# One V piece of the last block requested in two parts, 119 and 9 partitions, in a one-core attention decode kernel

## The chip, the cores and the metric

The kernel runs on one core of a Trainium2 chip. The time is that of the device for one execution, in microseconds, as the median of the runs. A core has TensorE (PE, matrix products; PEld is its weight load), VectorE (DVE), ScalarE (ACT), GpSimd (POOL) and SyncE (SP), which here only issues DMA requests. The requests are carried out by 16 DMA engines, which all move packets from HBM to SBUF, the on-chip memory of 128 partitions.

## The reference

One token attends over a cache of 65,536 positions: 8 heads of K and V, each with 2 query heads, 256 elements per head, bf16. A small gated mixer over the same token is added. Cut to what matters:

```python
q = (x @ wq).reshape(B, Sq, Hq, Dh)                    # 16 heads of 256
scores = einsum("bhqd,bhkd->bhqk", q, k) * Dh ** -0.5  # k, v: 8 heads x 65536 x 256
p = softmax(scores)
a = einsum("bhqk,bhkd->bhqd", p, v).reshape(...) @ wo  # 4096 -> 448
g = sigmoid((x * gate_w).sum(-1))
out = g * a + (1 - g) * mixer(x)
```

K and V together are 537 MB, and each byte is used once per query pair.

## The kernel before

The cache is cut into 32 blocks of 16,384 positions (`NBLK`; four to each K/V head). In a block, partition p holds 128 consecutive positions (`VP`), so a K or V block is 128 partitions x 64 KB, 8 MB. For each block the kernel loads K, transposes it on VectorE (`transposes`, L410), multiplies it with the queries (`scores`, L418), makes the softmax of the block with a running maximum (`softmax`, L475 to L514), and multiplies the probabilities, transposed in `pT`, with V (`pv`, L438). Blocks 0 to 29 run in a loop of 15 rounds with two blocks each (L605); each round also loads and uses the output weights Wo of one head. Blocks 30 (`L - 1`) and 31 (`L`) stand behind the loop, written out.

All large requests are issued by SyncE, in program order (`seq` pins the order on each engine). The 16 DMA engines take them up in that order. Each request counts up one of eight completion counters, taken in turn; before a request is issued, the former request on its counter must have landed.

For the last block, V doesn't go to its usual buffer `vt`, which still holds block 30, but to the K slots that have come free (`v_half`). It is requested by `load_v_last` (L158 to L164) in seven pieces of falling size, all 128 partitions wide: rows j = 0 to 63 of each partition, then 64 to 95, 96 to 111, 112 to 119, 120 to 123, 124 and 125, 126 and 127. A row is 256 bf16, 512 bytes. Behind them SyncE requests the last Wo tile (`load_wo`, L152) and, at the very end, writes the output (L705).

What uses this V: the lower half (j below 64) goes through `pv` into `pv_last` (L438). The upper half goes through `columns` (L463), which makes for each j two products with V as the stationary operand, one for each half of the head's columns, into `hd_ps`. `columns(64, 80)` comes first, then eight products that add the accumulated rest (L684), then `columns(80, 128)`. With the four rows of the changed piece (j = 120 to 123) go eight of these products. Behind them follow a scaling on VectorE (L691), eight products with Wo (L697; the second four use the Wo tile of L152), two copies (L703, L704) and the output.

Of the kernel before, what the change touches and what calls it, by code (L numbers as in the profile page):

```python
# [21 lines left out]
KP = VP // 2  # L22
# [11 lines left out]
def kernel(  # L34
# [15 lines left out]
    nc = tc.nc  # L50
# [12 lines left out]
    def seq(ins):  # L63
        e = ins.ins.engine
        if e in last:
            tc.add_manual_dep(
                ins.ins,
                last[e],
                mybir.DependencyInfo(
                    mybir.DependencyClass.NoSync, mybir.DependencyReason.DATA  # L70
                ),
                reason="program order",
            )
        last[e] = ins.ins.name
        return ins
# [47 lines left out]
    def rows(name, n):  # L123
        return flat[name][bass.ds(n, 1)].rearrange("o p j d -> (o p) j d")
# [15 lines left out]
    v_half = [slots[0], slots[2]]  # L140
    LAST = ((0, 64), (64, 96), (96, 112), (112, 120), (120, 124), (124, 126), (126, 128))

    def load_wo_wide(h):
        seq(nc.sync.dma_start(
            out=wo_in[0:128:WS],
            in_=A_wo.rearrange("(h q c) n -> h q c n", q=128 // WS, c=WC)[bass.ds(h, 1)].rearrange(
                "o q c n -> (o q) c n"
            ),
        ))
# [8 lines left out]

    def load_v_last(n):
        for j0, j1 in LAST:  # L160
            seq(nc.sync.dma_start(
                out=v_half[j0 // KP][:, j0 % KP:(j1 - 1) % KP + 1, :],
                in_=rows("v", n)[:, j0:j1, :],
            ))  # L164

    seq(nc.scalar.dma_start(out=xr[:], in_=A_x[0, 0].rearrange("(o n) -> o n", o=1)))
    seq(nc.sync.dma_start(
        out=wq_t[:, :], in_=A_wq[DM:D, :].rearrange("r (h n) -> (r h) n", h=2)
# [8 lines left out]
    for n0, n1 in ((0, D // 2), (D // 2, D)):  # L177
        seq(nc.scalar.dma_start(
            out=gw[:, n0:n1], in_=gate_w.rearrange("(o n) -> o n", o=1)[:, n0:n1]
# [14 lines left out]
        out=val[:], in_=rowsel[:, :, :, 0:NI], op=ALU.add, axis=AXIS.XY  # L194
    ))
    fst = const.tile([128, 2, REP], FP32)
    for e in range(2):
        seq(nc.vector.tensor_reduce(
            out=fst[:, e, :], in_=rowsel[:, :, :, e:e + 1], op=ALU.add, axis=AXIS.XY
# [3 lines left out]
        out=par[:], in_=ident_f[:].rearrange("p (a r) -> p r a", r=REP), op=ALU.add, axis=AXIS.X  # L203
# [3 lines left out]
        out=nval[:], in0=val[:], scalar1=-scale, scalar2=None, op0=ALU.mult  # L207
# [7 lines left out]
        out=same[:], in_=val[:].unsqueeze(1).to_broadcast([128, 64, REP])  # L215
# [8 lines left out]
        out=sel[:],  # L224
        in_=ident.rearrange("p (w k) -> p w k", w=NW).unsqueeze(2).to_broadcast([128, NW, NQ, 32]),
# [7 lines left out]
        out=xrr[:], in_=xr[:, DM:D].unsqueeze(2).to_broadcast([1, D - DM, 2])  # L233
    ))
    x_col = hd_ps[:, 40:44]
    for k in range(3):
# [13 lines left out]
        out=xtm[:], in0=par[:], scalar1=x_col[:, 3:4], scalar2=None, op0=ALU.mult  # L250
# [19 lines left out]
        out=veps[:], in0=mv[:, 1:2], scalar1=1e-5, scalar2=None, op0=ALU.add  # L270
# [5 lines left out]
    for _ in range(2):  # L276
# [3 lines left out]
            out=ntmp[:], in0=ntmp[:], scalar1=-0.5, scalar2=1.5, op0=ALU.mult, op1=ALU.add  # L280
# [3 lines left out]
        out=h_bc, in0=xf, scalar1=mv[:, 0:1], scalar2=rstd[:, 0:1],  # L284
        op0=ALU.subtract, op1=ALU.mult,
    ))
    for b in range(NF):
        seq(nc.scalar.activation(
            out=gel[b], in_=h_bc, func=ACT.Gelu_apprx_tanh,
# [33 lines left out]
    for k in range(2):  # L323
        seq(nc.vector.tensor_copy(
            out=qq[:, :, :, k, :], in_=qq_ps.rearrange("p (w g r) -> p w g r", g=HKV, r=REP)
# [279 lines left out]
    with tc.For_i(0, HQ - 1, 1, iteration_sync="staggered") as t:  # L605
        for e in range(2):
            if e:
                tc.stage_boundary()
            if e == 0:
                spread_wo(1)  # L610
                head_end()
                older_wo()
            tc.previous_stage_wait(mybir.EngineType.Activation)
            score_block(
                e, (e, e + 1), early_signals(0), FORWARD if e else UPPER_FIRST
            )
            load_v(2 * t + e)
            tc.stage_boundary()
            if e == 0:
                load_k_whole(2 * t + 1, 1)  # L620
                load_wo_wide(t)
                softmax(e, may_begin=True)
                tc.previous_stage_wait(mybir.EngineType.DVE)
                tc.previous_stage_wait(mybir.EngineType.Activation)
                products(e)
            else:
                load_k_whole(2 * t + 2, 0)
                softmax(e, pair=t + 1)
                tc.previous_stage_wait(mybir.EngineType.DVE)
                tc.previous_stage_wait(mybir.EngineType.Activation)  # L630
                denominators()
                turn()
                products(e)
# [6 lines left out]
    for n in (L - 1, L):  # L640
# [4 lines left out]
        if n == L - 1:  # L645
            load_v(n, 0, 48)
            load_k(L, 0, 2)
            load_k(L, 1, 1)
            load_v(n, 48, VP)
        else:  # L650
            load_v_last(L)
            load_wo(HQ - 1, 1)
        if n < L:
            softmax(n % 2)
        else:
            def rest_base():
# [9 lines left out]
                out=lsv[:], in0=val[:], scalar1=lsum[:, 0:1], scalar2=None, op0=ALU.mult  # L666
# [8 lines left out]
                out=rdv[:], in0=rdv[:], scalar1=gcol[:, 0:1], scalar2=None, op0=ALU.mult  # L675
# [6 lines left out]
    for c in range(2):  # L682
# [9 lines left out]
        out=oT[:], in0=o_last, in1=rdv[:].unsqueeze(1).to_broadcast([128, 2, REP]), op=ALU.mult  # L692
# [43 lines left out]
```

## Time and profile before

| | us |
|---|---|
| median of 3 runs | 1264.28 (1263.87 to 1925.72) |
| span of the profiled execution | 1261.8 |
| PE busy | 824.5 (65%) |
| DVE busy | 711.8 (56%) |
| HBM read | 544.22 MB, 431 GB/s over the span |

The span goes from the first to the last instruction of the profiled execution. The queue q1 carries SyncE's requests, q10 those of ScalarE, and q8 and q14 fetch instructions.

### The profile page before, as it was taken

Reading aid. Unit: us, or ns where it says so; the run is one execution under the profiler, and the core shown is the slowest. Engines: PE = TensorE matmul, PEld = TensorE weight load, DVE = VectorE, ACT = ScalarE, POOL = GpSimd, SP = SyncE. Lnnn points to the kernel's source line nnn. Section 1 sums busy time; section 2 is a strip of 40 time slices with the busy share of each in tenths; the row PEclk is TensorE's granted clock in tenths of the full one; section 3 lists DMA queues with packets and bytes.
Section 4 is the critical chain, followed back from the end, with each engine's and each line's share of the span. In section 5 each row is a group of like instructions: output and inputs, shape, how many; then the busy total and the mean of one; then the engine's idle time right before and its main releaser. Section 6 shows DMA issues by size and latency. Waiting matters only on the chain.

```text
span 1261.8 us, 12358 instructions
## 1 busy us (share of the span) xinstructions
PE 824.5 (65%) x4818; PEld 331.2 (26%) x4818; DVE 711.8 (56%) x755; ACT 75.7 (6%) x163; POOL 4.8 (0%) x9
## 2 busy tenths in 40 slices
PE   4757467575666756577566766658656576665668
PEld 2222122222222312223222322223222232222224
DVE  5665456654556644566544665445655456654575
ACT  4000000000000000000000000000000000000000
POOL 1000000000000000000000000000000000000000
PEclk8887788877787877978778887788877797877878
DMA  9999999999999999999999999999999999999998
GB/s 415 435 435 432 439 432 432 437 434 437 432 434 435 434 425 440 416 441 443 423 434 437 432 432 439 432 439 432 432 439 432 439 432 432 439 432 435 421 435 355
DMA packets 11624, 544.36 MB, mean 431 GB/s; under 512 B 1532, under 2 KB 1918, under 8 KB 2782
## 3 DMA queue, kind: packets, MB, share of 16 engines
q1 hardware_dynamic: 11522, 544.22, 99.6%
q8 instruction: 6, 0.10, 0.0%
q14 instruction: 4, 0.03, 0.0%
q10 hardware_dynamic: 92, 0.01, 0.0%
HBM read 544.22 MB, written 0.00 MB: 431 GB/s over the span
## 4 chain that ended last, share of the span: by engine, by line
DMA 67%; PE 14%; DVE 13%; issue 4%; ACT 0%; SPq 0%; DVEq 0%; ACTq 0%
DMA k_all<-in_A_k_cache_dram 67%; PE sc L418 13%; DVE kT L410 13%; PE hd_ps L463 0%; PE pv_last L438 0%; PE pv_last L563 0%; PE f L563 0%; DVE rmax L475 0%; PE hd_ps L684 0%; ACT p_sb L506 0%; PE hd_ps L554 0%; PE pv_ps L438 0%; PE f L697 0%; PE sm_ps L493 0%; DVE pT L513 0%
## 5 line engine op out<-in xcount | busy, mean ns | idle before, releaser
L418 PE MATMUL sc<-kT,qz 128*128 128x512 bf16 x2048 | 550.4, 419 | 315.0 <-DVE kT L410 314.8
L410 DVE STREAM_TRANSPOSE kT<-k_all 128x2048 f32<-128x2048 f32 x256 | 571.3, 2283 | 207.6 <-DMA k_all<-in_A_k_cache_dram 154.7
L418 PEld LDWEIGHTS <-qz 128*128 128x128 bf16 x2048 | 212.5, 104 | 651.3 <-issue 474.8
L438 PE MATMUL pv_ps<-vt,pT 128*4 128x512 bf16 x1968 | 172.0, 525 | 27.3 <-DVE pT L513 27.3
L519 DVE SCALAR_TENSOR_TENSOR acc<-acc,al,pv_ps 128x512 f32<-128x512 f32 x31 | 23.2, 747 | 160.4 <-PE pv_ps L438 160.4
L438 PEld LDWEIGHTS <-pT 128*4 128x4 bf16 x2000 | 56.5, 108 | 130.1 <-issue 83.9
L506 ACT ACTIVATE p_sb<-sc,nb 128x512 bf16<-128x512 f32 x32 | 22.0, 687 | 1020.0 <-DVE nb L502 1020.0
L475 DVE TENSOR_REDUCE rmax<-sc 128x1 f32<-128x512 f32 x32 | 22.1, 692 | 63.7 <-PE sc L418 63.7
L513 DVE STREAM_TRANSPOSE pT<-p_sb 128x512 bf16<-128x512 bf16 x32 | 22.8, 712 | 27.1 <-ACT p_sb L506 27.1
L525 PE MATMUL hd_ps<-lsum,same 128*128 128x1 f32 x30 | 8.2, 342 | 28.8 <-DVE lsum L514 28.8
L493 PE MATMUL sm_ps<-mrun,ones_f 1*128 1x2 f32 x64 | 12.1, 256 | 21.2 <-DVE mrun L492 13.0
L479 PE MATMUL sm_ps<-ident_f,rmax 128*1 128x128 f32 x32 | 8.6, 270 | 24.5 <-DVE rmax L475 24.5
L563 PE MATMUL pv_last<-wo_in,steps 128*128 128x448 bf16 x64 | 15.6, 368 | 5.5 <-PEq L605 5.5
L563 PEld LDWEIGHTS <-steps 128*128 128x128 bf16 x128 | 11.6, 101 | 22.6 <-issue 14.4
L493 PEld LDWEIGHTS sm_ps<-mrun,ones_f 1*128 1x128 f32 x64 | 9.4, 182 | 27.4 <-DVE mrun L492 16.3
L567 ACT CAST wo_sb<-pv_last 128x448 bf16<-128x448 f32 x16 | 8.5, 532 | 126.3 <-PE pv_last L563 126.3
L558 DVE TENSOR_TENSOR a_acc<-a_acc,hd_ps 1x448 f32<-1x448 f32 x15 | 9.1, 608 | 12.3 <-PE hd_ps L554 12.3
L554 PE MATMUL hd_ps<-wo_sb,oT 128*1 128x448 bf16 x60 | 15.8, 351 | 0.0
L563 PE MATMUL f<-wo_in,steps 128*128 128x448 bf16 x64 | 15.5, 367 | 0.0
L570 ACT COPY wo_sb<-wo_sb 128x896 bf16<-128x896 bf16 x15 | 14.1, 937 | 14.5 <-PE hd_ps L554 14.5
L525 PEld LDWEIGHTS hd_ps<-lsum,same 128*128 128x128 f32 x30 | 6.9, 285 | 30.1 <-DVE lsum L514 30.1
L550 DVE CAST oT<-hd_ps 128x2 bf16<-128x2 f32 x15 | 2.4, 160 | 20.8 <-PE hd_ps L540 20.8
(124 smaller groups left out, 194.6 us busy)
## 6 DMA issues: line engine op xcount, KB each, us to landing
k_all<-in_A_k_cache_dram SPq DMA_DIRECT2D x2, 4096.0 KB, 15.2
vt<-in_A_v_cache_dram SPq DMA_DIRECT2D x1, 5120.0 KB
k_all<-in_A_v_cache_dram SPq DMA_DIRECT2D x1, 4096.0 KB
wo_in<-in_A_wo_dram SPq DMA_DIRECT2D x15, 224.0 KB, 27.8
vt<-in_A_wq_dram SPq DMA_DIRECT2D x1, 3072.0 KB, 10.4
vt<-in_A_v_cache_dram SPq DMA_DIRECT2D x1, 3072.0 KB
k_all<-in_A_v_cache_dram SPq DMA_DIRECT2D x1, 2048.0 KB
k_all<-in_A_v_cache_dram SPq DMA_DIRECT2D x1, 1024.0 KB, 21.7
```

The source lines that it names most:

```text
L410: seq(nc.vector.transpose(out=kT_tiles[i % 2][:].rearrange("p j w k c -> p (j w k c)").bitcast(FP32), in_=slots[pair[i // 4]][:, i % 4 * N ...
L418: seq(nc.tensor.matmul(sc_tiles[e][:, :], lhsT=qz[:, 2 * w + c, 2 * (NI - i):2 * (NI - i) + 128], rhs=kT_tiles[i % 2][:, :, w, :, c], star ...
L438: seq(nc.tensor.matmul(dst[32 * grp:32 * grp + 2 * REP, :, :], lhsT=pT[:, 32 * jj + 2 * REP * ip:32 * jj + 2 * REP * (ip + 1)], rhs=pairs( ...
L475: seq(nc.vector.tensor_reduce(out=rmax[:], in_=sc_ps[:, :], op=ALU.max, axis=AXIS.X))
L493: seq(nc.tensor.matmul(sm_ps[:, 128:128 + REP], lhsT=ones_f[0:1, :], rhs=mrun[0:1, :], start=True, stop=True))
L506: seq(nc.scalar.activation(out=p_sb[:, :], in_=sc_ps[:, :], func=ACT.Exp, scale=scale, bias=nb[:, 0:1], accum_out=den[:, 0:1],))
L513: seq(nc.vector.transpose(out=pT[:, :], in_=p_sb[:, :]))
L519: seq(nc.vector.scalar_tensor_tensor(out=acc[:], in0=acc[:], scalar=al_tiles[e][:, 0:1], in1=src[:, :, :], op0=ALU.mult, op1=ALU.add,))
L525: seq(nc.tensor.matmul(hd_ps[:, 460:461], lhsT=same[:].rearrange("p a r -> p (a r)"), rhs=lsum[:, 0:1], start=True, stop=True,))
L554: seq(nc.tensor.matmul(a_ps, lhsT=oT[:, c, r:r + 1], rhs=wo_sb[:, r, c, :], start=(r == 0 and c == 0), stop=(r == REP - 1 and c == 1),))
L563: seq(nc.tensor.matmul(wo_ps[c], lhsT=steps[:, WS - u:WS - u + 128], rhs=wo_in[:, 2 * u + c, :], start=(u == 0), stop=(u == WS - 1),))
L570: seq(nc.scalar.copy(out=wo_sb[:, 0], in_=wo_sb[:, 1]))
```

## The change

The piece of rows j = 120 to 123 is requested in two parts, partitions 0 to 118 and partitions 119 to 127. The other six pieces, all destinations and all computations are the same. The rows of the piece so land under two completion counters, and the requests behind it use the next counter each.

```diff
     LAST = ((0, 64), (64, 96), (96, 112), (112, 120), (120, 124), (124, 126), (126, 128))
 
+    PARTS = {120: ((0, 119), (119, 128))}
+
...
     def load_v_last(n):
         for j0, j1 in LAST:
-            seq(nc.sync.dma_start(
-                out=v_half[j0 // KP][:, j0 % KP:(j1 - 1) % KP + 1, :],
-                in_=rows("v", n)[:, j0:j1, :],
-            ))
+            for p0, p1 in PARTS.get(j0, ((0, 128),)):
+                seq(nc.sync.dma_start(
+                    out=v_half[j0 // KP][p0:p1, j0 % KP:(j1 - 1) % KP + 1, :],
+                    in_=rows("v", n)[p0:p1, j0:j1, :],
+                ))
```

## The prediction

> **What bounds the kernel now.** I read the page first: its span, the row of DMA busy shares, the queues and the shares of the chain.
>
> ```profile
> span 1261.8 us, 12358 instructions
> DMA  9999999999999999999999999999999999999998
> ...
> q1 hardware_dynamic: 11522, 544.22, 99.6%
> ...
> q10 hardware_dynamic: 92, 0.01, 0.0%
> ...
> DMA 67%; PE 14%; DVE 13%; issue 4%; ACT 0%; SPq 0%; DVEq 0%; ACTq 0%
> ```
>
> The 16 DMA engines are busy in every slice, and 544.22 MB take the whole span. The kernel is bound by the stream of K and V, except in the last microseconds, where what the last bytes allow must still be computed. The change touches one of the last requests of that stream, so only the end can move. The span is 1261.8 us and the median of the runs 1264.28 us: 2.5 us lie outside the first and the last instruction, and the change doesn't touch them. Of the three runs two lie 0.41 us apart (1263.87 and 1264.28); the third, 1925.72 us, is no measure of this change.
>
> Next, the chain of waits in order of time, its last 12 us:
>
> ```profile
> 1250.37 0.71 DVE pT L513
> ...
> 1251.88 1.83 PE pv_last L438 x32
> 1253.71 0.89 PE hd_ps L463 x32
> 1254.60 1.07 PE hd_ps L684 x8
> 1255.67 2.55 PE hd_ps L463 x96
> 1258.22 0.02 issue
> 1258.25 0.17 DVE oT L691
> 1258.42 0.04 issue
> 1258.46 0.95 PE f L697 x8
> 1259.42 0.37 DVE res L703
> ```
>
> No DMA stands in it. From pT on, TensorE goes from step to step without a wait that the chain shows. The 96 products of L463 (`columns(80, 128)`, two to a V row j) include the eight for j = 120 to 123, whose rows are the changed piece. The timeline gives their pace, and the start of the very last one:
>
> ```profile
> 1255.53 2.68 PE L463 MATMUL hd_ps<-pT,k_all 128*128 128x2 bf16 x96
> ...
> 1258.05 0.17 PE L463 MATMUL hd_ps<-pT,k_all 128*128 128x2 bf16 x1
> 1258.46 0.91 PE L697 MATMUL f<-wo_sb,oT 128*1 128x224 bf16 x8 [0.25 <-DVE oT L691]
> ```
>
> One product lasts 0.17 us and they overlap: (2.68 - 0.17) / 95 = 26.4 ns from one to the next. At that pace the four products of the last piece (j = 126, 127) start from 1258.05 - 3 x 0.026 = 1257.97 us, and the eight of the changed piece from 1258.05 - 15 x 0.026 = 1257.65 us. Now when the data is there: SyncE's issues of V, and their time to landing (the answer for L161).
>
> ```profile
> 1219.79 17.87 SPq L161 DMA_DIRECT2D k_all<-in_A_v_cache_dram  x7
> 1238.31 0.33 SPq L152 DMA_DIRECT2D wo_sb<-in_A_wo_dram  x1
> ...
> L161 SPq DMA_DIRECT2D k_all<-in_A_v_cache_dram x7: 327/328/424, 1219.8 to 1237.2; - x7
> ...
> DMA to landing us min/median/max: 20.7/21.2/21.7
> ```
>
> The last V request is issued at 1237.2 us, and with 20.7 us it lands at 1257.9 us, some 0.07 us before TensorE comes to it. So two chains end together: the V stream and TensorE's products. This decides the whole forecast: V that comes earlier gains next to nothing, and V that comes later by more than 0.07 us costs its full lateness.
>
> Last, the stages of the tail (columns: stretch, length, busy time and count of PE, PEld, DVE, ACT and POOL, granted clock, DMA share, GB/s):
>
> ```profile
> 1252.00:1254.00 2.00, 2.00 (x46) 0.93 (x39) 0.68 (x4) 0.00 (x0) 0.00 (x0) 1.00 0.97 410
> ...
> 1255.00:1256.00 1.00, 1.00 (x25) 1.00 (x25) 0.00 (x0) 0.00 (x0) 0.00 (x0) 0.91 1.06 403
> 1256.00:1257.00 1.00, 1.00 (x43) 1.00 (x41) 0.00 (x0) 0.00 (x0) 0.00 (x0) 0.50 0.85 312
> 1257.00:1258.00 1.00, 1.00 (x44) 1.00 (x42) 0.00 (x0) 0.00 (x0) 0.00 (x0) 0.50 0.37 134
> 1258.00:1259.00 1.00, 0.75 (x16) 0.44 (x13) 0.16 (x1) 0.00 (x0) 0.00 (x0) 0.50 0.01 4
> ```
>
> In the microsecond to 1256 all 16 engines work; in the one to 1258 the share is 0.37, about 6 of 16. The engines don't finish together: most are done near 1256.5, and some six run on to about 1258. Those late engines set the 1257.9.
>
> **The change, part by part.** It replaces one request (128 partitions, 4 rows of 512 B each, 256 KB) by one of 119 partitions and one of 9. The bytes and their order stay. Everything before the last V requests is the same instruction for instruction, so the loop's time stays.
>
> *One more issue on SyncE.* Two requests of L161 back to back show its price:
>
> ```profile
> 1236.77 0.90 SPq L161 DMA_DIRECT2D k_all<-in_A_v_cache_dram  x2
> ```
>
> Two took 0.90 us, of which one lasts 0.42, so one more costs 0.48 us. It moves the last two V requests from 1236.8 and 1237.2 to about 1237.3 and 1237.7, with about 20 us to go until they land; the queue before them hides it. Without that cover it would cost 0.48 us.
>
> *The completion counters move by one.* The requests take eight counters in turn, and a request waits until its counter's former user has landed. With one request more, the last V request takes over the wait for `vt` that Wo had, and Wo waits instead for the first half of the last V block:
>
> ```profile
> SPq L161 <- DVE kT L410: 22.8, 4, 9.7
> ...
> SPq L152 <- DMA vt<-in_A_v_cache_dram: 0.6, 1, 0.6
> ```
>
> ```profile
> vt<-in_A_v_cache_dram SPq DMA_DIRECT2D x1, 5120.0 KB
> k_all<-in_A_v_cache_dram SPq DMA_DIRECT2D x1, 4096.0 KB
> ```
>
> The last V request so goes out at about 1238.3 us (when Wo goes now), 1.1 us later than now and still 19 us early. Wo (L152) waits for the half block of 4096 KB. The pieces behind that half are another 4096 KB, 4.19 MB at 410 to 430 GB/s = 9.8 to 10.2 us, so it lands about 10 us before 1257.9, near 1248. Wo is then issued near 1248.2 instead of 1238.3, some 8 us before the first engines run out of V (1256). Hidden; without that cover Wo would come as late as its issue is late. Behind it on SyncE stands only the output, issued at 1259.9.
>
> *The spread over the engines.* This is the one part with an open answer. The queue rows above count packets, and the requests can be read from the code: on SyncE 15 rounds of four 128-row requests and one of 32 rows, 15 more 128-row requests (three ahead of the loop, twelve behind it) and the output; on ScalarE three of 14 rows and four of one row. If each request has a packet for every row and one completion for every engine that it runs on, 16 for 128 and for 32 rows, 14 for 14 rows and one for one row, the counts come out exactly: 15 x (4 x 144 + 48) + 15 x 144 + 2 = 11522, and 3 x 28 + 4 x 2 = 92. So 128 and 32 rows run on 16 engines, 14 rows on 14, one row on one. No request of 119 or 9 rows is in the trace. One packet of the piece is 2 KB; at 410 / 16 = 25.6 GB/s it takes an engine 0.080 us. Now it is 8 packets, 0.64 us, for each of 16 engines. The bounds:
>
> - All 16 engines share the 119 rows: each has 7 to 9 packets, the end moves by at most 0.08 us.
> - One engine carries the 119 rows: 111 packets more, 8.9 us later.
> - Some of the engines carry them, with the late ones among those or not: between a small gain and the rival below.
>
> I take the first end's value, about 0: rows of 128, 32 and 14 all use as many engines as they can, and between even and uneven spreads the late engines decide, which no view names. What can be gained if the late engines are relieved is bounded by TensorE, which has no gap from 1255.53 to 1258.2: V gives 0. Wo, the last bytes of all, feeds the second half of the eight products of L697; at most part of their 0.91 us is waiting, and one product alone takes under 0.4, so under 0.5 us; I take 0.1. The eight products of the changed piece wait for two counters instead of one, a step that other products do without a gap that the timeline shows: 0 to 0.1 us.
>
> [...]
>
> The sum: 0 for V, 0 to -0.1 for Wo, 0 to +0.1 for the second counter: 1264.3 us.
>
> **The rivals.**
>
> *Slower: the added packets fall on late engines.* If the 119 rows go to few engines, say seven with 17 packets, and one of the late six is among them, it carries about 10 packets more, 10 x 0.080 = 0.80 us. V would land at 1257.9 + 0.8, TensorE has 0.07 us to spare, so the end moves by about 0.7 us: 1265.0 us. It decides as soon as an engine that now ends after about 1257.2 gets the packets. For it: about six engines run to nearly 1258, and nothing seen keeps them out of any set of seven. Against it: the engines done by 1256.5 can carry 0.8 us more and still end before 1257.4. [...]
>
> *One engine carries it all.* 111 packets more, 8.9 us, less up to 1.4 us of an early engine: 1264.3 + 7.4 to 8.8, about 1272 us. The packet counts speak against it: only one-row requests use one engine.
>
> *Faster: the late engines are relieved and Wo counts.* Up to 0.5 us off the eight last products: 1263.8 us. Against it: the first four of them don't need Wo and start only at 1258.46, after nearly all bytes have passed (share 0.01 after 1258).
>
> *The change does nothing at all* (an even spread) gives the forecast's number.
>
> **How the numbers follow.** The forecast, 1264.3, has 0.50; the late engines loaded 0.38 (1265.0); the gain 0.08 (1263.8); one engine 0.03 (1272); 0.01 for something else. The first three differ by 1.2 us together. To them come the 0.41 us between runs and the 2.5 us outside the span, which I can't watch; half of those on the lower side and a little more on the upper give 1262.3 to 1266.3, and the case of one engine is left out. About 2%, 25 us, is what a measurement of this kernel can tell from no change; no case reaches it, so "within 2%" has 0.98 and either side 0.01.
>
> **What would show it.** In the changed kernel the packets of q1 tell the spread: seven and nine engines give 11522 - 144 + 126 + 18 = 11522 again, 16 and nine engines 11531, one and nine 11516. The busy share from 1256 to 1258 tells who got the packets: flatter, with the stream's end before 1257.7, if the late engines were relieved; a thin tail to about 1258.7, with idle time before products of L463, if they were loaded. The 96 products must stay near 2.68 us for the forecast. SyncE must issue Wo near 1248 and nobody wait for that. Wrong would be above all a tail of several microseconds, or a loop that changes its time.

## The result, and the profile after

| | median, us | runs | lowest to highest |
|---|---|---|---|
| before | 1264.21 | 21 | 1263.29 to 1925.72 |
| changed | 1265.85 | 21 | 1264.91 to 1266.60 |

The changed kernel takes 1.0014 of the time before, 95% interval [1.0008, 1.0019]: between 1.0 and 2.4 us more. The medians of the table differ by 1.64 us; three runs of before (1566.17 to 1925.72 us) are disturbed, and without them its median is 1263.88 us and the difference 1.97 us. That is far within 2%, and still clear: beside those three, only one run of before, 1265.87 us, is as long as any of the changed kernel. The profiled execution of the changed kernel took 1264.91 us, the least of its 21 runs, and has a span of 1263.1 us, 1.3 us more than before.

The chain of waits in the changed kernel, by time (start, length, what), is short, because it meets a DMA request:

```profile
1236.42 22.16 DMA k_all<-in_A_v_cache_dram
1258.58 0.14 issue
1258.72 0.71 PE hd_ps L466 x16
1259.42 0.02 issue
1259.45 0.17 DVE oT L694
1259.62 0.04 issue
1259.67 0.95 PE f L700 x8
1260.62 0.37 DVE res L706
```

Before, no DMA stood in the last 12 us, and the products of `columns(80, 128)` (then L463, now L466) ran from 1255.53 to 1258.2 without a gap. Now the request issued at 1236.42, the part of 9 partitions, lands at 1258.58, and sixteen products wait for it. They are the eight of the changed piece and the eight of the two pieces behind, and the last four start when the last piece has landed, at 1259.10 by its counter (1257.90 before). The timeline shows two gaps (in brackets: idle time and what ended it):

```profile
1254.87 1.75 PE L466 MATMUL hd_ps<-pT,k_all 128*128 128x2 bf16 x64
...
1257.25 0.59 PE L466 MATMUL hd_ps<-pT,k_all 128*128 128x2 bf16 x16 [0.64 <-DMA k_all<-in_A_v_cache_dram]
...
1258.72 0.70 PE L466 MATMUL hd_ps<-pT,k_all 128*128 128x2 bf16 x16 [0.88 <-DMA k_all<-in_A_v_cache_dram]
```

The second gap is the changed piece (j = 120 to 123) with the four rows behind it. The first is the piece ahead of it (j = 112 to 119), whose request wasn't touched. By the counters it landed at 1257.20, where it landed at 1256.67 before, while the piece ahead of that one landed at nearly the same time (1255.51 and 1255.43): something slows the stream beyond the changed request. Beside that, TensorE came to the piece 0.66 us earlier than before; at the former time it would have found the piece just landed, and this gap wouldn't stand here. The stages (last two columns: DMA share, GB/s; a packet counts where it starts, so a share can pass 1.00) show the slower stream too:

```profile
1255.00:1256.00 1.00, 1.00 (x47) 1.00 (x44) 0.00 (x0) 0.00 (x0) 0.00 (x0) 1.00 1.07 393
1256.00:1257.00 1.00, 0.61 (x25) 0.53 (x21) 0.00 (x0) 0.00 (x0) 0.00 (x0) 0.71 0.74 218
1257.00:1258.00 1.00, 0.59 (x16) 0.51 (x16) 0.00 (x0) 0.00 (x0) 0.00 (x0) 0.50 0.59 204
1258.00:1259.00 1.00, 0.28 (x11) 0.32 (x12) 0.00 (x0) 0.00 (x0) 0.00 (x0) 0.50 0.22 80
```

The tail has moved: from 1257 to 1259 the share is 0.59 and 0.22, where it was 0.37 and 0.01. From 1256 to 1257 a share of 0.74 moves 218 GB/s, where 0.85 moved 312: 295 GB/s for a full share, where it was 367. The engines are not only busy later, they get less done while they are busy. An instruction fetch starts in this stretch in both kernels, with 0.08 and 0.06 of the share, which doesn't make up the difference; the lengths of single packets, below, show it directly.

The queue row tells how the rows were dealt out:

```profile
q1 hardware_dynamic: 11522, 544.22, 99.6%
```

11522 again: 126 + 18 packets in place of 144, so 119 rows ran on seven engines and 9 rows on nine, if each engine gives one completion, as every count of before has it. The counters of the two requests bear that out: seven landings on the first, nine on the second. Of the nine, two come at 1255.16 and 1255.38 and seven from 1257.10 to 1258.58, as they would if the seven engines with the 119 rows were among the nine.

### The profile page after: what moved, and what is told of

Same layout as the page of the kernel before. It is cut to its first block, busy times and chain, and to the rows that moved or that the text cites. A ratio compares the mean times of both kernels' runs of the same rounds, so it can differ in the third digit from the quotient of the medians.

```text
span 1263.1 us, 12360 instructions
## 1 busy us (share of the span) xinstructions
PE 825.8 (65%) x4818; PEld 331.7 (26%) x4818; DVE 711.5 (56%) x755; ACT 75.6 (6%) x163; POOL 4.8 (0%) x9
## 3 DMA queue, kind: packets, MB, share of 16 engines
q1 hardware_dynamic: 11522, 544.22, 99.6%
## 4 chain that ended last, share of the span: by engine, by line
DMA 68%; PE 13%; DVE 12%; issue 4%; SPq 0%; ACT 0%; DVEq 0%
DMA k_all<-in_A_k_cache_dram 67%; PE sc L421 13%; DVE kT L413 12%; DMA k_all<-in_A_v_cache_dram 2%; PE pv_last L566 0%; PE f L566 0%; PE hd_ps L557 0%; PE f L700 0%; ACT p_sb L509 0%; PE hd_ps L466 0%; SPq L164 0%; DVE rmax L478 0%; SPq L132 0%; PE hd_ps L543 0%; PE sm_ps L543 0%
## 5 line engine op out<-in xcount | busy, mean ns | idle before, releaser
L441 PE MATMUL pv_ps<-vt,pT 128*4 128x512 bf16 x1968 | 175.1, 533 | 27.3 <-DVE pT L516 27.3
L566 PEld LDWEIGHTS <-steps 128*128 128x128 bf16 x128 | 11.6, 100 | 22.6 <-issue 14.4
```

Of the source, the lines that this page charges most:

```text
L441: seq(nc.tensor.matmul(dst[32 * grp:32 * grp + 2 * REP, :, :], lhsT=pT[:, 32 * jj + 2 * REP * ip:32 * jj + 2 * REP * (ip + 1)], rhs=pairs( ...
L566: seq(nc.tensor.matmul(wo_ps[c], lhsT=steps[:, WS - u:WS - u + 128], rhs=wo_in[:, 2 * u + c, :], start=(u == 0), stop=(u == WS - 1),))
```

## The experiments

Three theories stood after the result. **A**: engines that are late anyway get more packets. **B**: a request of fewer than 128 partitions makes packets longer, whoever carries them. **C**: one request more, and shifted counters, cost something by themselves. Kernels run together share the runs of before; the intervals are those of the ratio to it. The edits are to the lines of the change, and `PARTS` has only the piece named; the last three variants edit the request of the first piece itself, and the remarks behind `#` are no part of the edits.

**An even split.**

```diff
-    PARTS = {120: ((0, 119), (119, 128))}
+    PARTS = {120: ((0, 112), (112, 128))}
```

> The piece split as 112 and 16 partitions: still one request more and the counters shifted as in the changed kernel, but 7 + 1 packets for each of 16 engines, as many as before. Theory A (late engines carry more packets): as before, within 0.2 us. Theory B (a split makes engines write partitions that other engines write, and packets get longer): 0.3 to 0.6 us slower than before, with 2 KB packets above 84 ns on average. Theory C (one request more, shifted counters): about 1.6 us slower, like the changed kernel.

Measured: 1264.92 us against 1263.96, ratio 1.0007 [0.9998, 1.0017]. The interval just reaches no change, but the runs don't overlap (1264.57 to 1265.20 against 1263.35 to 1264.32). Theory A alone falls: with both parts on 16 engines, 8 packets for each as before by an estimate (112 / 16 + 16 / 16), 0.96 us are lost, more than the 0.3 to 0.6 that theory B had given. The stages:

```profile
1255.00:1256.00 1.00, 1.00 (x23) 1.00 (x23) 0.00 (x0) 0.00 (x0) 0.00 (x0) 1.00 1.03 338
1256.00:1257.00 1.00, 1.00 (x47) 1.00 (x44) 0.00 (x0) 0.00 (x0) 0.00 (x0) 1.00 1.07 313
```

All engines are busy to 1257 and move 338 and 313 GB/s, where the kernel before moved 403 from 1255 to 1256 and the split by rows, below, 374 from 1256 to 1257. The timeline shows what that does to the products:

```profile
1257.81 0.56 PE L466 MATMUL hd_ps<-pT,k_all 128*128 128x2 bf16 x16 [0.45 <-DMA k_all<-in_A_v_cache_dram]
1258.65 0.62 PE L466 MATMUL hd_ps<-pT,k_all 128*128 128x2 bf16 x16 [0.29 <-DMA k_all<-in_A_v_cache_dram]
```

The same two gaps stand ahead of the same products as in the changed kernel, only shorter: 0.45 and 0.29 us, where they were 0.64 and 0.88. The queue row says that all 16 engines had both parts:

```profile
q1 hardware_dynamic: 11538, 544.22, 99.6%
```

11538 is 11522 + 16: the same 128 rows, and 16 completions for each of the two parts. The packet records of the trace give the mean length of a packet, in ns, from 1246 us on:

```text
kernel                 4 KB   2 KB   1 KB
before                  159     84     46
changed (119 + 9)       167     95     48
112 + 16                177     94     54
64 + 64                 182    100     58
120 + 8                 182     97     57
127 + 1                 159     84     52
two by rows             159      -     46
```

Before, all packets of one of these sizes last the same to the nanosecond; after a split by partitions among several engines they stretch in the mean (2 KB: 94 to 100 ns in place of 84), those of the neighbouring pieces too (4 KB: 167 to 182 in place of 159; 1 KB: 48 to 58 in place of 46). The row 127 + 1 is told below.

**The same number of requests, split by rows.**

```diff
-    LAST = (... (112, 120), (120, 124), (124, 126), (126, 128))
+    LAST = (... (112, 120), (120, 122), (122, 124), (124, 126), (126, 128))
```

> [...] Theory B (a request of fewer than 128 partitions gives engines other partitions, and their packets collide with those of neighbours): as before within 0.3 us, packets at their usual length (46 ns for 1 KB). Theory C (one request more, shifted counters) about 1.0 us slower, like the even split by partitions.

Measured: 1264.11 us against 1264.17, ratio 0.9999 [0.9990, 1.0008], packets at their usual length (159 and 46 ns for 4 and 1 KB). The queue row and two stages:

```profile
q1 hardware_dynamic: 11666, 544.22, 99.6%
```

```profile
1255.00:1256.00 1.00, 1.00 (x32) 1.00 (x33) 0.00 (x0) 0.00 (x0) 0.00 (x0) 1.00 1.01 377
1256.00:1257.00 1.00, 1.00 (x42) 0.97 (x39) 0.00 (x0) 0.00 (x0) 0.00 (x0) 0.89 1.03 374
```

There is a whole request's 144 packets more, and in the stretches where the even split moved 338 and 313 GB/s, 377 and 374 go through. Theory C falls: a request more and the shifted counters cost nothing that can be measured, though the interval alone would allow up to 1.0 us. What costs is the split by partitions.

**Two more splits by partitions.**

```diff
+    PARTS = {120: ((0, 64), (64, 128))}
...
+    PARTS = {120: ((0, 120), (120, 128))}
```

> [...] Theory B: 0.6 to 1.3 us slower, 2 KB packets of 90 ns or more on average. Theory A alone (load): as before. Theory C: about 1.0 us.

> [...] If an engine's partitions in a full request are eight neighbours, 15 of 16 engines keep theirs here: theory B then gives 0.1 to 0.3 us (one packet more, few collisions). If its partitions lie elsewhere, packets get longer as in the even split: about 1 us. Theory C: about 1.0 us.

Measured: 1265.27 us for 64 + 64 and 1265.15 us for 120 + 8, both against 1264.17, both ratios 1.0008 [0.9999, 1.0017], so each interval just reaches no change. Each again loses about 1 us (1.10 and 0.98) and stretches packets (2 KB: 100 and 97 ns in place of 84). So it is not the number 112. And 120 rows on 15 engines, by the packet count (11529 = 11522 - 144 + 128 + 15 + 8), stretch them as well. If it matters which engine writes which partition, as theory B has it, a full request is then hardly dealt in groups of eight neighbours, or 15 of the 16 engines would have kept theirs; that is argued, not shown.

**Which engines are late.**

```diff
+    PARTS = {120: ((0, 112), (112, 119), (119, 128))}
```

The request of 7 rows is there for its landings, which stand on a counter of their own.

> [...] Theory B: 0.3 to 0.6 us slower. Theory C: two requests more, about 3 us slower.

Measured: 1265.26 us against 1263.96, ratio 1.0012 [1.0003, 1.0021], 1.3 us more than before and 0.3 us over the even split; that is more than the 0.3 to 0.6 us of theory B, also with one packet more on an engine, 0.08 us, beside it. The completions of the 7-row request, one for each engine, by the trace's counter, in us:

```text
1255.82 1256.07 1256.08 1256.97 1257.67 1257.69 1258.16
```

Three engines of the seven are early, one is late by 1.2 us and three by 1.9 to 2.3 us. That is theory A's other half: the late engines are not kept out of the seven that had the 119 rows (17 each if dealt evenly, 119 / 7, an estimate), if the 7-row request runs on the same seven, which the trace doesn't name. The changed kernel fits it: of the sixteen landings of its last piece four stand apart at the end, 1258.46 to 1259.10, behind a gap of 0.46 us. Before, six ended together, from 1257.44 to 1257.90. The stretched packets are in these numbers too, so the lateness is somewhat overstated.

**One engine for the whole piece.**

```diff
+    PARTS = {120: ((0, 127), (127, 128))}
```

> [...] Theory A: 120 packets more on one engine at 0.08 us, 9.6 us, less up to 1.8 us if that engine is among the early ones, plus 16 products behind: 7.5 to 10 us slower than before. If the rows were spread over 16 engines: 1 us, like the even split.

Measured: 1272.11 us against 1264.02, ratio 1.0063 [1.0047, 1.0080], 8.1 us more. The packets of q1 and the stages:

```profile
q1 hardware_dynamic: 11508, 544.22, 99.0%
```

```profile
1255.00:1256.00 1.00, 1.00 (x46) 1.00 (x44) 0.00 (x0) 0.00 (x0) 0.00 (x0) 1.00 0.52 213
...
1257.00:1258.00 1.00, 0.43 (x16) 0.34 (x14) 0.00 (x0) 0.00 (x0) 0.00 (x0) 0.89 0.07 27
```

11508 = 11522 - 144 + 128 + 2: 127 rows, one completion. From 1257 a single engine runs on at 27 GB/s, with a share of 0.07 where one of 16 engines is 0.06, and its 2 KB packets last 84 ns, the usual, from 1255.27 to 1265.43, although other engines work beside it at both ends of that time; the 4 KB packets beside it keep their 159 ns too. So theory B doesn't hold "whoever carries them": carried by one engine, the packets of the split piece don't stretch. The loss lies in the 7.4 to 8.8 us that the prediction had for one engine. One thing more shows here: SyncE's issue of the one-row part, behind the 127-row request, took 21.3 us where the others take 0.3 to 0.4, so the last two pieces were issued only at 1257.33 and 1257.74. Their 1 KB packets, nearly all moved in one burst from 1258.32, last 52 ns in the mean and up to 279. That didn't set the end: the last landing of those pieces is at 1266.51, 1.1 us behind the last 2 KB packet, as it would be if the one engine has its share of them behind its 127 packets.

**Smaller and larger pieces, split 119 + 9.**

```diff
+    PARTS = {126: ((0, 119), (119, 128))}
...
+    PARTS = {112: ((0, 119), (119, 128))}
```

> The last piece (2 rows, packets of 1 KB) split as 119 and 9 partitions in place of the 4-row piece. Theory A: 10 packets of 0.043 us more on late engines, 0.43 us, and only 4 products wait for it: 0.3 to 0.6 us slower than before, a third of the changed kernel's loss. Theory B: longer packets too, 0.5 to 0.9 us. Theory C: 1.6 us, as the request count is the same.

> The 8-row piece (j = 112 to 119, packets of 4 KB) split as 119 and 9 partitions in place of the 4-row piece. Theory A: 10 packets of 0.156 us more, 1.56 us, and 32 products (0.9 us) wait for it, less the 1.1 us that the piece lands before TensorE's end: 1.5 to 2.4 us slower than before. Theory B adds 0.5 to 1 us for longer packets: 2.0 to 3.4 us. Theory C: 1.6 us.

Measured against 1263.96: the 2-row piece 1264.92, ratio 1.0008 [0.9999, 1.0017]; the 8-row piece 1267.44, ratio 1.0028 [1.0017, 1.0040]. So 2, 4 and 8 rows lose 0.96, 1.97 and 3.48 us: the loss grows with the bytes of the piece, as both A and B ask and C doesn't. Both new pieces lie a little above what A and B together gave (0.5 to 0.9 and 2.0 to 3.4).

**A long piece, evenly split.**

```diff
+    PARTS = {0: ((0, 112), (112, 128))}
```

> The first piece (64 rows, 4 MB) split as 112 and 16 partitions, even load, the 4-row piece whole. Theory B: the collisions last for the whole piece; if it loses what the even split of the small piece loses in its stretch (338 in place of 403 GB/s), 4 MB take 12 in place of 10 us: 1 to 2.5 us slower than before. If only the requests around the change of partitions suffer: 0.3 to 1 us. Theory C: about 1.0 us.

Measured: 1277.13 us against 1264.17, ratio 1.0097 [1.0082, 1.0112]: 13 us, five times what theory B had given as its most. The stages of the piece, which before runs at 413 to 440 GB/s:

```profile
1240.00:1245.00 5.00, 4.20 (x19) 1.63 (x17) 4.74 (x3) 0.00 (x0) 0.00 (x0) 1.00 0.96 257
...
1250.00:1255.00 5.00, 1.16 (x18) 0.45 (x10) 1.85 (x6) 0.00 (x0) 0.00 (x0) 0.92 1.09 154
1255.00:1260.00 5.00, 0.00 (x0) 0.08 (x1) 0.00 (x0) 0.00 (x0) 0.00 (x0) 0.50 0.86 118
```

With the engines nearly always busy (shares of 0.96 and 1.09) the 112 rows move at 257 GB/s, and the end of them with most of the 16 rows at 154. The last stretch, at 118, is mostly the next piece: by the packet records 0.52 of the 0.59 MB that start there are packets of 16 KB, of j = 64 to 95, which is requested whole. The first 112 packets of 32 KB to start last 2.2 us in the median, the last sixteen 3.3 to 4.3, where it was 1.21 before; the 16 KB packets of the next piece last up to 2.3 us, where they lasted 0.61.

**Which side collides.** Three variants of the long piece ask whether the rows that are read or the partitions that are written make the difference. The first sends it to partitions 0 to 111 and 112 to 127 in two requests, as the long split does, but the first request reads the first seven rows of each group of eight and the second the eighth. Rows of V so land in other partitions than the products take them for, which changes the output and not the amount of work.

```diff
+        groups = rows("v", n)[:, 0:64, :].rearrange("(e r) j d -> e r (j d)", r=8)   # to partitions 0:112 and 112:128
...
+            in_=rows("v", n)[:, 0:64, :].rearrange("(a b) j d -> b a (j d)", b=16),   # one request, rows shuffled
...
+                    in_=A_v_cache[0, HKV - 1][SK - 128 * 67:SK] ...                    # 112 + 16, rows 33.5 KB apart
```

> [...]

> The first piece (4 MB) as one request of 128 partitions, with the rows of V read in a shuffled order (partition 8 b + a takes row 16 a + b). Rows of V so land in other partitions than the products take them for, which changes the output and no amount of work. If the collisions are on the side of SBUF and a full request keeps its partitions: as before within 0.5 us. If the order of reading from HBM decides: several us slower. If the shuffled side makes the request be dealt out like one of fewer partitions: about 10 us slower too, and the two sides stay unseparated.

> The first piece (4 MB) split as 112 and 16 partitions, which cost 13 us, but each partition reads its 32 KB from rows that lie 33.5 KB apart (67 positions) in place of 64 KB apart. The first piece so holds other rows of V than the reference takes, which changes the output and no amount of work. If the stretched packets come from the partitions that are written together (SBUF): 10 to 14 us slower than before, as with the usual rows. If they come from addresses 64 KB apart that are read together (HBM): 0 to 2 us slower, packets of 32 KB back at 1.21 us. The 32-row Wo request of the loop, which reads dense rows, is never stretched in the kernel before (480 packets of 272 ns), which speaks for HBM.

Measured: the first 1276.66 us against 1264.02, ratio 1.0095 [1.0078, 1.0112]; the second 1275.62, ratio 1.0093 [1.0076, 1.0109]; the third 1277.14 against 1264.22, ratio 1.0096 [1.0079, 1.0113]. The first and the third in stages:

```profile
1240.00:1245.00 5.00, 4.50 (x21) 1.84 (x20) 4.93 (x3) 0.00 (x0) 0.00 (x0) 1.00 0.94 236
...
1255.00:1260.00 5.00, 0.00 (x0) 0.08 (x1) 0.00 (x0) 0.00 (x0) 0.00 (x0) 0.56 0.92 125
```

```profile
1240.00:1245.00 5.00, 4.50 (x20) 1.82 (x19) 4.93 (x3) 0.00 (x0) 0.00 (x0) 1.00 0.92 236
...
1255.00:1260.00 5.00, 0.00 (x0) 0.08 (x1) 0.00 (x0) 0.00 (x0) 0.00 (x0) 0.51 0.87 141
```

The first and the third read other rows in other places and write the same partitions in the same two requests, and both lose the 13 us of the long split. The distance of the rows in HBM, which the expectation of the third leaned to, is not the cause. Every kernel with these two requests loses alike, whatever rows they read, so the cost goes with the two requests and the partitions that they write. The shuffled request leaves a doubt, and its own case for that came true: the two sides aren't separated by it. It writes all 128 partitions at once and loses 11.6 us, and its 32 KB packets last 1.8 to 2.9 us, 2.5 in the mean. So writing only a part of the partitions is not what stretches packets in every case. Its shuffled side has 16 groups of 8 rows, so it may be dealt to the engines in another way than a plain one of 128; no run here shows how. Which partitions each engine writes was not seen either.

## Why the prediction was right and wrong

- **The number, 1264.3, in a range from 1262.3 to 1266.3.** The measured 1265.85 lies in the range and within 2%. The likeliest case was not the one that came: the rival "the added packets fall on late engines" (0.38, 1265.0 us) did, with a second cost beside it that no part of the sum had. That the range held it is luck as far as the mechanism goes: its width came mostly from the 2.5 us outside the span, taken from the median of one set of runs and the span of one execution, and the executions of the changed kernel have 1.7 to 2.0 us there. Its upper end is also not what the working gives: 1266.3 lies 1.3 us above 1265.0, which is less than half of the 2.9 us and not a little more.
- **"I take the first end's value, about 0."** Here it failed. The rows were not spread over 16 engines; the packet count, named ahead as the test, says seven and nine. That 128, 32 and 14 rows use 16, 16 and 14 engines didn't carry over to 119. No run of before shows the seven engines with 17 packets that the rival's "about 10 packets more" is worked out from; it was the author's estimate. The runs show seven landings for the 119 rows here, and 11508 packets for 127 + 1 (one engine for each part) and 11538 for 112 + 16 (16 engines for each). The prediction had this case as a rival, with its price, and still put more on the even spread.
- **"All 16 engines share the 119 rows: ... the end moves by at most 0.08 us."** This bound was wrong in itself. It counted packets at their usual length. The even split, with as many packets as before for each engine by the estimate above, loses 0.96 us, and its 2 KB packets last 94 ns in place of 84.
- **The price of the rival, 0.7 us, against 1.6 to 2.0.** The difference between 119 + 9 and the even split, each against its own runs of before, is 1.97 - 0.96 = 1.01 us (0.68 by the 1.64 of the table), where the rival had 0.7. It is an estimate, since the two splits don't stretch packets alike. So the load was sized to within about 0.3 us, and the rest, about 1 us, is the longer packets.
- **"V that comes later ... costs its full lateness."** Right: the last piece of V landed 1.20 us later (1259.10 for 1257.90), and the products ended 1.21 us later (1259.43 for 1258.22), 0.3 us behind that landing in both kernels. The wait for 1258.58 that the chain shows isn't the one that set the end.
- **The issue, the counters and Wo, costed at nothing.** Right: the split by rows has them all and takes the time of before. Wo was issued where the sum put it (near 1248.2), and nobody waited for it; nor did Wo give anything, as the eight last products take 0.91 us in both kernels:

```profile
1248.21 0.33 SPq L154 DMA_DIRECT2D wo_sb<-in_A_wo_dram  x1
```

- **"V gives 0" for the gain.** Not tested, as no run brought V earlier.

## What to carry to other kernels

A request of all 128 partitions could here be cut by rows within the partitions at no cost that could be measured, but not by partitions: even the 112 rows of the long split ran at 236 to 257 GB/s where the whole ran at over 400, and the loss grew with the bytes (0.96, 1.97 and 3.48 us for 2, 4 and 8 rows). Count the packets of a queue: here rows plus one completion for each engine accounted for every count (11522, 11508, 11529, 11538, 11666), and so told how many engines a request ran on. Where TensorE and the stream end within 0.1 us of each other, as here, a later landing of the last piece is lost in full (1.20 us of landing, 1.21 us of products); what an earlier one would give was not tested.

## What the runs showed of the hardware

In the tail of the kernel before, from 1246 us on, where all requests of V are full, their packets of one size last the same to the nanosecond (84 ns for 2 KB). When a request to a part of the partitions runs on several engines they last up to 3.6 times as long (4.4 in place of 1.21 us for 32 KB), and the packets of full requests running beside it stretch with them (up to 2.4 in place of 0.61 us for 16 KB). A full request whose rows are shuffled on the HBM side stretches its packets too (2.5 us in the mean for 32 KB). The 127 rows on one engine keep the usual 84 ns.

The last sixteen packets of 32 KB, most of them of the 16 rows that go to partitions 112 to 127, take 3.9 to 4.0 us in the mean in the three long splits; sixteen at once would move 16 x 32 KB / 3.9 us = 134 GB/s, an estimate, a third of the 413 to 440 GB/s at which the piece runs before. The sixteen packets didn't all run at once. Why the first 112 packets of 32 KB took 1.8 times as long as before in the median (2.2 us in place of 1.21) isn't explained by any run here.
